# Fused attention and Fourier-mixing kernel: V's two signs in one tile, heads in natural order, stores as steps of their own, and a new order of work

## The chip, the cores and the metric

The kernel runs on one core of a Trainium2 chip, in one launch. A core has five engines with queues of their own: TensorE (PE, with its weight loads shown as PEld), VectorE (DVE), ScalarE (ACT), GpSimd (POOL) and SyncE (SP). SP, ACT and POOL also issue DMAs. Each engine works through its own queue in the order in which the program was written, and waits for others by semaphores. The metric is the device time of one execution, in microseconds (us), lower is better; what is compared is the median of several runs.

## What is computed

Inputs are q, k and v, each 8 batches x 8 heads x 576 rows x 64, a projection `w_phi` (64 x 128), and two feed-forward weights (512 x 2048 and 2048 x 512), all fp32.

```python
def phi(x):
    proj = np.einsum('bhsd,df->bhsf', x, w_phi)
    proj = proj - np.max(np.abs(proj), axis=-1, keepdims=True)
    return np.concatenate([np.exp(proj), np.exp(-proj)], axis=-1)
q_p, k_p = phi(q), phi(k)
kv = np.einsum('bhsf,bhsd->bhfd', k_p, v);  z = np.sum(k_p, axis=2)
num = np.einsum('bhsf,bhfd->bhsd', q_p, kv)
den = np.einsum('bhsf,bhf->bhs', q_p, z)[..., None] + 1e-06
x = num / den, heads side by side: (8, 576, 512)

mixed = np.real(np.fft.fft(np.fft.fft(x, axis=1), axis=2))
u = x + mixed
un = (u - mean(u)) / sqrt(var(u) + 1e-06)          # over the last axis
out = u + np.maximum(un @ w_ch1, 0.0) @ w_ch2
```

So each batch goes through four parts: feature maps of k and q, linear attention, the real part of a two-dimensional Fourier transform, and a normalised feed-forward network.

## The kernel before

Every batch is a set of small generators ("streams"), each of which issues a few instructions per step. `STREAMS` gives each a letter and a number of steps; the string `PLAN` is the order written out by hand or by a planner: each letter issues the next step of that stream, for its own next batch. So PLAN fixes the order on every engine's queue at once, and steps of neighbouring batches stand interleaved. A step holds instructions of several engines, its DMAs included. Below, `M1.19` means step 19 of stream M for batch 1.

The streams:

- `K`, `V`, `Q` (`fetch_*`, issued on POOL) load a batch of k, v and q, cast to bf16. `B` and `A` (`arrive_k`, `arrive`, on SP) turn k and q by DMA transposes into `KT` and `QT`. Batch 0 instead loads fp32 on SP and turns it on TensorE (`G`, `J`).
- `T` (18 steps; 20 for batch 0) projects k and q (PSUM tiles `psk`, `psh`, `ps`) and exponentiates on ACT into `KPp`, `KPn` (exp(proj), exp(-proj) of k) and `QPHP`, `QPHN`. `R` takes on DVE the maxima of |proj| of k, into `MK` and, for the last 64 rows, `MK4`; `P` those of q into `MQ`.
- `S` puts the factors exp(+max), exp(-max) of k into V: ACT writes the exponential into column 64 of the tile (L438, L424), and POOL multiplies V by it (L443, L428). `VCn`, `VCp` hold the two signs for the first 512 rows, `V4N`, `V4P` for the last 64: one multiply a sign and pair of heads.
- `M` is attention and mixing: `keyvalue` for eight heads (PSUM tile `kv`, ten matmuls a head, then ACT's cast to `kvh`, L861); `combine` for eight heads (TensorE, DVE, and L975 on POOL into `X`); the two Fourier matmul stages (`psD`, then `pu`) with DVE's folded sums into `CEO` between them (L1007, in steps M.17 and M.19); and the sums X + mixed (L1077). `D` folds `X` on DVE before that (L869 to L893).
- `N` normalises: DVE's statistics, ACT's centred bf16 `UN`, then an SP DMA transpose to `UT` (in batch 0 by TensorE). `U` computes 1/sigma (POOL, L1173).
- `F` (68 steps) is the feed-forward network: 128 hidden matmuls (`psf`, L1207) with ACT's Relu eviction into `HT`, then `output` for the five row blocks (`pso`, L1224, L1250), DVE's scaled sum into `X`, and the store.
- `C`, `H` make the Fourier constants, `Z` pads, `W` loads the two weights, `Y` (`stir`) issues filler matmuls in the first part.

The first 512 rows of an X tile lie as four blocks of 128 rows, and c = 4 holds the last 64. The store of a block (`store`, L1180) is called straight after DVE's sum of that block inside `output`:

```python
            nc.vector.scalar_tensor_tensor(
                out=U[:, c, 0:C], in0=po[:], scalar=scale_of[b, c], in1=U[:, c, 0:C], ...
            )
            store(b, U, c)
```

c = 1 stores blocks 0 and 1 by four DMAs on SP's queue, which is also the queue of the transposes of `KT`, `QT` and `UT`.

Heads are taken in pairs, for batch 0 in the order `PAIRS = (0, 3, 2, 1)`, and combined in the order 0, 1, 6, 7, 4, 5, 2, 3. The first two steps of `D` fold `X` by column quarters: first quarters 0 and 3, then 1 and 2.

In batch 0 the q maxima are not applied as a factor afterwards but subtracted inside the projection: `turn_m` (L692) splits 20 maxima a row into three bf16 parts (four small DVE operations), turns them by one matmul, and copies them out of PSUM.

## Time and profile before

| | us |
|---|---|
| median of three runs (lowest, highest) | 416.78 (416.39, 419.95) |
| the profiled execution, its own time | 415.15 |
| its span, first to last instruction | 413.4 |
| TensorE busy in the span | 394.6 (95%) |
| DVE / ACT / POOL busy | 319.4 / 303.8 / 215.1 |
| first hidden-layer matmul of batch 0 | 50.9 |
| last DMA issue (SP) | 408.05 |

The profile is of one execution. "Busy" of TensorE is modelled, as matmuls are pipelined. In a row of groups the columns are: line, engine, operation, output and inputs, shape, count; total busy us and mean ns of one; and idle time ahead of it with what ended it. In a row of waits: engine and line that waited, what ended the wait; total us, times, longest. In a row of the timeline: start, duration, engine, line, operation, and in brackets the idle time before. In a table of stretches, each engine's busy us stands with its instruction count in brackets, and the last columns are granted clock, DMA share and GB/s.

### The profile page before, as it was taken

Reading aid. Unit: us, or ns where it says so; the run is one execution under the profiler, and the core shown is the slowest. Engines: PE = TensorE matmul, PEld = TensorE weight load, DVE = VectorE, ACT = ScalarE, POOL = GpSimd, SP = SyncE. Lnnn points to the kernel's source line nnn. Section 1 sums busy time; section 2 is a strip of 40 time slices with the busy share of each in tenths; the row PEclk is TensorE's granted clock in tenths of the full one; section 3 lists DMA queues with packets and bytes.
Section 4 is the critical chain, followed back from the end, with each engine's and each line's share of the span. In section 5 each row is a group of like instructions: output and inputs, shape, how many; then the busy total and the mean of one; then the engine's idle time right before and its main releaser. Section 6 shows DMA issues by size and latency. Waiting matters only on the chain.

```text
span 413.4 us, 10526 instructions
## 1 busy us (share of the span) xinstructions
PE 394.6 (95%) x4194; PEld 259.5 (63%) x4194; DVE 319.4 (77%) x662; ACT 303.8 (73%) x617; POOL 215.1 (52%) x279
## 2 busy tenths in 40 slices
PE   7898999989999989999899999999999999999994
PEld 3574577535856568566756577566856586658563
DVE  5979887999699867797689878888799768875101
ACT  6988999658958886688868886789758885544350
POOL 8997695774466753707658373649271343201000
PEclk9999899999999999999999999999999999999999
DMA  7999979898674899654965979757952141106103
GB/s 210 221 170 158 181 100 185 87 118 128 102 118 58 67 179 141 63 92 83 129 97 65 156 104 142 80 72 116 117 97 52 46 83 21 27 14 114 24 23 90
DMA packets 108520, 42.71 MB, mean 103 GB/s; under 512 B 82615, under 2 KB 103479, under 8 KB 108471
## 3 DMA queue, kind: packets, MB, share of 16 engines
q0 software_dynamic: 46272, 16.60, 37.1%
q1 hardware_dynamic: 61703, 24.85, 32.9%
q10 hardware_dynamic: 496, 0.59, 0.6%
q8 instruction: 33, 0.54, 0.5%
q14 instruction: 16, 0.13, 0.1%
HBM read 36.77 MB, written 9.44 MB: 112 GB/s over the span
## 4 chain that ended last, share of the span: by engine, by line
PE 69%; DVE 13%; DMA 8%; ACT 4%; POOL 3%; issue 2%; DVEq 0%; POOLq 0%; SPq 0%; ACTq 0%
PE psf L1207 29%; PE pso L1224 19%; DMA UT<-UN 4%; PE kv L853 3%; PE psD L1035 2%; PE psk L468 2%; DMA KT<-KS 2%; PE pu L1087 2%; DMA KS<-in_k_dram 2%; PE psq L522 2%; PE psh L563 1%; DVE MK L488 1%; PE pso L1250 1%; DVE cb L969 1%; DVE X L1077 1%
## 5 line engine op out<-in xcount | busy, mean ns | idle before, releaser
L1207 PE MATMUL psf<-UT,W1b 128*128 128x320 bf16 (+1 forms) x1024 | 141.1, 286 | 2.9 <-DMA UT<-UN 2.8
L1224 PE MATMUL pso<-W2b,HT 128*128 128x512 bf16 x496 | 120.5, 379 | 0.0
L1207 PEld LDWEIGHTS <-W1b 128*128 128x128 bf16 x1024 | 94.6, 98 | 30.9 <-issue 3.8
L1212 ACT ACTIVATE HT<-psf 128x320 bf16<-128x320 f32 x128 | 53.9, 444 | 25.7 <-PE psf L1207 19.5
L1224 PEld LDWEIGHTS <-HT 128*128 128x128 bf16 x496 | 45.2, 98 | 43.2 <-issue 0.4
L975 POOL TENSOR_TENSOR X<-cb,rd 128x640 f32<-128x640 f32 x28 | 35.1, 1254 | 52.9 <-DVE rd L973 29.6
L443 POOL TENSOR_TENSOR VCn<-VS,VCn 128x512 bf16<-128x512 bf16 x28 | 29.9, 1067 | 43.4 <-ACT VCn L438 36.6
L530 DVE TENSOR_REDUCE MQ<-psq 128x8 f32<-128x1024 f32 (+1 forms) x32 | 34.3, 1088 | 17.8 <-PE psq L522 17.4
L1230 DVE SCALAR_TENSOR_TENSOR X<-pso,rs,X 128x512 f32<-128x512 f32 x31 | 23.0, 743 | 28.2 <-PE pso L1224 28.0
L1214 ACT ACTIVATE HT<-psf 128x512 bf16<-128x512 f32 x64 | 37.3, 602 | 6.8 <-PE psf L1207 6.6
L488 DVE TENSOR_REDUCE MK<-psk 128x8 f32<-128x1024 f32 x28 | 33.8, 1210 | 1.4 <-ACT KPn L474 1.4
L474 ACT ACTIVATE KPp<-psk 128x1024 bf16<-128x1024 f32 x28 | 28.8, 1027 | 7.8 <-PE psk L468 7.5
L258 POOL DMA_DIRECT2D QS<-in_q_dram x49 | 33.4, 688 | 1.1 <-issue 1.1
L1133 ACT ACTIVATE UN<-X,MV 128x512 bf16<-128x512 f32 (+1 forms) x35 | 25.2, 726 | 11.5 <-DVE MV L1158 8.0
L572 ACT ACTIVATE QPHP<-psh 128x1024 bf16<-128x1024 f32 x28 | 28.9, 1031 | 4.8 <-PE psh L563 4.5
L474 ACT ACTIVATE KPn<-psk 128x1024 bf16<-128x1024 f32 x28 | 28.7, 1025 | 1.7 <-DVE MK L488 1.6
L443 POOL TENSOR_TENSOR VCp<-VS,VCp 128x512 bf16<-128x512 bf16 x28 | 29.9, 1067 | 0.0
L572 ACT ACTIVATE QPHN<-psh 128x1024 bf16<-128x1024 f32 x28 | 29.0, 1036 | 0.0
L1157 DVE BATCH_NORM_STATS2 st<-X 128x6 f32<-128x512 f32 (+1 forms) x40 | 27.1, 678 | 0.2
L1077 DVE TENSOR_TENSOR X<-pu,X 128x512 f32<-128x512 f32 (+3 forms) x49 | 23.5, 526 | 4.6 <-PE pu L1087 4.5
L955 PEld LDWEIGHTS <-QPHP 128*128 128x128 bf16 x280 | 20.5, 99 | 7.8 <-DVE cb L969 3.8
L1173 POOL TENSOR_TENSOR rs<-VE,mhalf 128x5 f32<-128x5 f32 (+1 forms) x9 | 10.3, 1148 | 24.8 <-DVE VE L1172 24.7
(462 smaller groups left out, 797.2 us busy)
## 6 DMA issues: line engine op xcount, KB each, us to landing
out_dram<-X SPq DMA_DIRECT2D x31, 128.0 KB
out_dram<-X SPq DMA_DIRECT2D x15, 256.0 KB
KS<-in_k_dram POOLq DMA_DIRECT2D x7, 512.0 KB, 8.2
VS<-in_v_dram POOLq DMA_DIRECT2D x14, 256.0 KB, 4.8
...
```

Source lines behind the costliest of these rows:

```text
L258: nc.gpsimd.dma_start(out=pieces[i][0], in_=pieces[i][1])
L443: nc.gpsimd.tensor_tensor(out=VC[:, hs, :, 0:D], in0=values[b][0][:, hs, :].rearrange("p h (j d) -> p h j d", d=D), in1=VC[:, hs, :, D:D + ...
L474: nc.scalar.activation(out=KP[:, hs, :, :].rearrange("p e (jp jj) f -> p jj (e jp) f", jj=2), in_=psk[:], func=AT.Exp, scale=sgn,)
L488: nc.vector.tensor_reduce(out=MK[:, 2 * pr:2 * pr + 2, :].rearrange("p e (jp jj) -> p jj (e jp)", jj=2), in_=tiles[pr][:], axis=AX.X, op=A ...
L530: nc.vector.tensor_reduce(out=o, in_=i[:], axis=AX.X, op=ALU.max, apply_absolute_value=True)
L572: nc.scalar.activation(out=o, in_=psh[:], func=AT.Exp, scale=sgn)
L975: nc.gpsimd.tensor_tensor(out=X[:, :, at:at + 2 * D].rearrange("p c (e d) -> p e c d", e=2), in0=cb[:, :, :, 0:D], in1=rd[:].to_broadcast( ...
L1077: nc.vector.tensor_tensor(out=to, in0=more, in1=to, op=ALU.add)
L1207: nc.tensor.matmul(ps, lhsT=W1b[:, cc, 128 * hh:128 * hh + 128], rhs=UT[:, cc, lo:hi], start=(cc == 0), stop=(cc == NCC - 1),)
L1212: nc.scalar.activation(out=HT[:, hh, lo:hi], in_=ps, func=AT.Relu, scale=-1.0)
L1214: nc.scalar.activation(out=HT[:, hh - 1:hh + 1, lo:hi], in_=psw[:].rearrange("p (a n) -> p a n", a=2), func=AT.Relu, scale=-1.0,)
L1224: nc.tensor.matmul(po[:], lhsT=HT[:, hh, at:at + 128], rhs=W2b[:, hh, :], start=(hh == 0), stop=(hh == NHH - 1),)
```

## The change

1. **V's two signs.** `VCp` and `VCn` become one tile `VC` with a sign axis, `V4P` and `V4N` one tile `V4S`; `MK` and `MK4` get a sign axis too. DVE writes the maxima to sign 1, POOL writes their negatives to sign 0, one ACT exponential covers both signs, and one POOL multiply covers both signs of a pair of heads.
2. **`keyvalue`** uses one PSUM tile for two heads; ACT casts both at once after the second.
3. **Natural head order** in batch 0 and in `combine`; `D`'s first two steps fold column halves. The outer heads' exponentials in batch 0 become one instruction, not two.
4. **q maxima of batch 0** (`turn_m`): ACT copies the fp32 maxima to three places, TensorE transposes them, and DVE splits them into bf16 parts in PSUM.
5. **Rows of X** have 514 elements, not 513.
6. **Stores** become a stream `O` of four steps (five in batch 7), in the order of blocks 2, 1 (with 0), 3, 4.
7. **A new PLAN.** Among other moves: `K1.0` and `K1.1` come ahead of most of S of batch 0; `R1.2` comes before M0.19 instead of after M0.20; `W0.1` comes just before F0.0; S.1 of every later batch comes after M.19; `O` steps lie some steps behind the sums that they store.

The diff, cut:

```diff
-PAIRS = (0, 3, 2, 1)
+PAIRS = (0, 1, 2, 3)
...
-    V4P = const.tile([128, 4, 2, D + 1], BF16, name="V4P")
-    V4N = const.tile([128, 4, 2, D + 1], BF16, name="V4N")
+    V4S = const.tile([128, 2, 4, 2, D + 1], BF16, name="V4S")
...
-        xpool.tile([128, 5, C + 1], F32, tag="X", name=n)[:].rearrange("p a b -> p (a b)")
+        xpool.tile([128, 5, C + 2], F32, tag="X", name=n)[:].rearrange("p a b -> p (a b)")
...
+    def scaling(b, MK, MK4, VC):
+        V, V4_ = values[b]
+
+        def scale_v4():
+            nc.gpsimd.tensor_single_scalar(
+                out=MK4[:, 0], in_=MK4[:, 1], scalar=-1.0, op=ALU.mult
+            )
+            for e in range(2):
+                rr = slice(64 * e, 64 * e + 64)
+                nc.scalar.activation(
+                    out=V4S[rr, :, :, e, D], in_=MK4[rr], func=AT.Exp, scale=1.0
+                )
+                nc.gpsimd.tensor_tensor(
+                    out=V4S[rr, :, :, e, 0:D],
+                    in0=V4_[rr].unsqueeze(1).to_broadcast([64, 2, 4, D]),
+                    in1=V4S[rr, :, :, e, D:D + 1].to_broadcast([64, 2, 4, D]), op=ALU.mult,
+                )
+
+        def scale_v(pr):
+            if pr % 2 == 0:
+                h4 = slice(2 * pr, 2 * pr + 4)
+                nc.gpsimd.tensor_single_scalar(
+                    out=MK[:, 0, h4], in_=MK[:, 1, h4], scalar=-1.0, op=ALU.mult
+                )
+                nc.scalar.activation(
+                    out=VC[:, :, h4, :, D].rearrange("p s h j -> p s (h j)"),
+                    in_=MK[:, :, h4].rearrange("p s h j -> p s (h j)"), func=AT.Exp, scale=1.0,
+                )
+            hs = slice(2 * pr, 2 * pr + 2)
+            to = VC[:, :, hs].rearrange("p s h j d -> p s (h j) d")
+            nc.gpsimd.tensor_tensor(
+                out=to[:, :, :, 0:D],
+                in0=V[:, hs, :].rearrange("p h (j d) -> p (h j) d", d=D).unsqueeze(1)
+                    .to_broadcast([128, 2, 8, D]),
+                in1=to[:, :, :, D:D + 1].to_broadcast([128, 2, 8, D]), op=ALU.mult,
+            )
...
         def turn_m(outer):
...
+            pt = pk.tile([96, 2, 128], F32, tag="pk", name="pt")
+            m = M0w[:, 1 - outer]
+            nc.scalar.copy(out=m[:, 1:3], in_=m[:, 0:1].to_broadcast([128, 2, 32]))
+            nc.tensor.transpose(pt[:, 0], m.rearrange("p i n -> p (i n)"), ident[:])
             mt_ = small.tile([96, 128], BF16, tag="mt", name="mt")
-            nc.vector.tensor_copy(out=mt_[:], in_=pt[:])
+            nc.vector.tensor_copy(out=mt_[:], in_=pt[:, 0])
+            nc.vector.tensor_tensor(
+                out=pt[0:64, 1], in0=pt[0:64, 0], in1=mt_[0:64], op=ALU.subtract
+            )
+            nc.vector.tensor_copy(out=mt_[0:64], in_=pt[0:64, 1])
+            nc.vector.tensor_tensor(
+                out=mt_[0:32], in0=pt[0:32, 1], in1=mt_[0:32], op=ALU.subtract
+            )
...
     def keyvalue(b, h):
...
+        if e == 0:
+            pool, tag = (pb, "pb") if b == 0 else (pk, "pk")
+            two_heads[b] = pool.tile([128, 2, 2, D + 1], F32, tag=tag, name="kv")
+        kv = two_heads[b][:, e]
...
+        if e:
+            kvh = work.tile([128, 2, 2, D + 1], BF16, tag="kvh", name="kvh", bufs=4)
+            nc.scalar.copy(out=kvh[:], in_=two_heads[b][:])
+            return kvh[:, 0], kvh[:, 1]
+        return ()
...
-        for cs in (slice(0, 4, 3), slice(1, 3)):
+        for cs in (slice(0, 2), slice(2, 4)):
...
-        for h in (0, 1, 6, 7, 4, 5, 2, 3):
+        for h in range(H):
             combine(h, kvh[h])
...
-            store(b, U, c)
             yield
...
+    def store_all(b):
+        U = turned_u[b][0]
+        for c in (2, 1, 3, 4) if b < B - 1 else (2, 1, 4):
+            store(b, U, c)
+            yield
+        if b < B - 1:
+            return
+        rows_ = out[b, 320:576, :].rearrange("(a r j) n -> a r j n", r=32, j=2)
+        for queue, at in ((nc.scalar, 0), (nc.sync, 256)):
             queue.dma_start(out=rows_[:, ::-1, 0, at:at + 256], in_=U[:, 3, at:at + 256])
             yield
```

More of the change, by code (lines that the diff above doesn't have):

```diff
@@ L243, in pads @@
             yield
-        for X_ in (V4P, V4N):
-            nc.gpsimd.memset(X_[:], 0.0)
+        for sgn in range(2):
+            nc.gpsimd.memset(V4S[:, sgn], 0.0)
             yield
@@ L339, in load_first, with half @@
         parts[0] = first_features()
+    def half(x, outer):
+        return x[:, 0:2] if outer else x[:, 2:4]
     def turn_part(dst, blocks, by_act):
@@ L679, in last_rows @@
             if sgn < 0:
-                for x, pr in enumerate((0, 3) if outer else (1, 2)):
+                for x, pr in enumerate((0, 1) if outer else (2, 3)):
                     for e in range(2):
@@ L721, in widest @@
                 nc.vector.tensor_reduce(
-                    out=half(by_pair(mq[:])[:, :, :, c], outer),
+                    out=M0[:, 1 - outer, :, :, c],
                     in_=ps[jj][:].rearrange("p (x e) f -> p x e f", e=2), axis=AX.X, op=ALU.max,
@@ L842, in first_features @@
+            for pr in range(4):
+                yield scale_v(pr)
         return maxima(), steps(), kmax(), scaled()
     def keyvalue(b, h):
-        KPp, KPn, K4p, K4n, VCp, VCn, _ = made[b]
+        KPp, KPn, K4p, K4n, VC, _ = made[b]
         pr, e = h // 2, h % 2
-        if b == 0:
-            kv = pb.tile([128, 2, D + 1], F32, tag="pb", name="kv")
-        else:
-            kv = pk.tile([128, 2, D + 1], F32, tag="pk", name="kv")
-        for i, (KP, K4, VC, V4) in enumerate(((KPp, K4p, VCp, V4P), (KPn, K4n, VCn, V4N))):
+        if e == 0:
+            pool, tag = (pb, "pb") if b == 0 else (pk, "pk")
+            two_heads[b] = pool.tile([128, 2, 2, D + 1], F32, tag=tag, name="kv")
@@ L857, in keyvalue @@
             nc.tensor.matmul(
-                kv[:, i, :], lhsT=K4[:, pr, :], rhs=V4[:, pr, e, :], start=False, stop=True
+                kv[:, i, :], lhsT=K4[:, pr, :], rhs=V4S[:, i, pr, e, :], start=False, stop=True
             )
-        kvh = work.tile([128, 2, D + 1], BF16, tag="kvh", name="kvh", bufs=8)
-        nc.scalar.copy(out=kvh[:], in_=kv[:])
-        return kvh
+        if e:
[3 more added lines that the diff above has]
+        return ()
     def folded(X, R, HI):
@@ L926, in first_heads @@
             for e in range(2):
-                kvh[2 * pr + e] = keyvalue(0, 2 * pr + e)
+                for x, made_ in enumerate(keyvalue(0, 2 * pr + e)):
+                    kvh[2 * pr + x] = made_
                 yield
-        for h in (0, 1, 6, 7):
+        for h in range(4):
             ps = pb.tile([128, 1, 512], F32, tag="pb", name="pn_")
@@ L941, in heads @@
             return (yield from first_heads())
-        KPp, KPn, K4p, K4n, VCp, VCn, E2 = made[b]
-        X = xpool.tile([128, 5, C + 1], F32, tag="X", name="X")
+        E2 = made[b][5]
+        X = xpool.tile([128, 5, C + 2], F32, tag="X", name="X")
         R = fpool.tile([128, 3, 2, 512], F32, tag="R", name="R")
@@ L1261, in forward @@
             )
-        store(b, U, 4)
         yield
@@ L1265, in forward @@
             return
-        rows_ = out[b, 320:576, :].rearrange("(a r j) n -> a r j n", r=32, j=2)
-        for queue, at in ((nc.scalar, 0), (nc.sync, 256)):
+        for at in (0, 256):
             po = pb.tile([128, 256], F32, tag="pb", name="pso")
```

178 lines of the change are left out of this document (50 added, 128 removed).

## The prediction

> **What bounds the kernel now.** I read the page's totals first, then busy time by stage. The stage bounds are the starts, in the chain of waits, of the first hidden-layer matmul of batch 0 (50.9), batch 1 (104.6) and batch 7 (375.8).
>
> ```profile
> PE 394.6 (95%) x4194; PEld 259.5 (63%) x4194; DVE 319.4 (77%) x662; ACT 303.8 (73%) x617; POOL 215.1 (52%) x279
> ```
> ```profile
> core 0: us, PE busy (x) PEld busy (x) DVE busy (x) ACT busy (x) POOL busy (x), PEclk, DMA share, GB/s
> 0.00:50.90 50.90, 44.07 (x493) 25.75 (x493) 42.27 (x103) 44.36 (x84) 43.01 (x75) 0.97 1.15 188
> 50.90:104.60 53.70, 51.53 (x582) 32.77 (x582) 48.70 (x101) 43.57 (x90) 37.16 (x44) 1.00 0.95 122
> 104.60:375.80 271.20, 267.28 (x2885) 179.31 (x2883) 221.22 (x448) 202.52 (x419) 133.76 (x160) 1.00 0.64 90
> 375.80:413.40 37.60, 31.70 (x240) 21.64 (x238) 7.25 (x15) 13.36 (x27) 1.17 (x1) 0.99 0.29 58
> ```
>
> From 104.6 to 375.8, six batches at 45.2 us, TensorE idles 271.20 - 267.28 = 3.92 us in all. The last stage is bare feed-forward matmuls. Their count is the same after the change, so what can move is the idle: 3.92 us here, 2.17 us from 50.9 to 104.6, and the start, where TensorE's busy time is partly the filler matmuls of `stir`. There ACT is busy 44.36 of 50.9 us, DVE 42.27 and POOL 43.01: three nearly full engines bound it. Matmul ends are modelled, so some waits may hide inside "busy"; that goes into the range.
>
> Then the waits, to see what the idle is (us in total, times, longest):
>
> ```profile
> PE psf L1207 <- DMA UT<-UN: 2.8, 4, 1.3
> PE psk L468 <- DMA KT<-KS: 1.8, 1, 1.8
> PE psD L1035 <- DVE CEO L1007: 1.2, 1, 1.2
> ...
> PE psD L1035 <- DVE CEO L1053: 0.4, 1, 0.4
> ...
> POOL VCn L443 <- ACT VCn L438: 36.6, 8, 12.5
> ...
> SPq L1184 <- DVE X L1230: 60.9, 6, 15.0
> ...
> SPq L1150 <- ACT UN L1133: 36.1, 7, 14.0
> ```
>
> TensorE waits for the transposed activations `UT` at four batch starts, for K once, and for DVE's `CEO` once. POOL, 52% busy, stands waiting for ACT's exponentials.
>
> **V's two signs in one tile.** Rows by form:
>
> ```profile
> L443 POOL TENSOR_TENSOR VCn<-VS,VCn 128x512 bf16<-128x512 bf16 x28 | 29.9, 1067 | 43.4 <-ACT VCn L438 36.6 <-issue 2.8 <-ACT VCp L438 2.7
> ...
> L428 POOL TENSOR_TENSOR V4N<-VS,V4N 64x256 bf16<-64x256 bf16 x14 | 8.7, 618 | 22.4 <-ACT V4N L424 18.5 <-PE psf L1207 3.4
> ...
> L438 ACT ACTIVATE VCn<-MK 128x16 bf16<-128x16 f32 x14 | 4.0, 287 | 0.4 <-DVE MK L488 0.3
> ...
> L424 ACT ACTIVATE V4N<-MK 64x4 bf16<-64x4 f32 x14 | 3.0, 216 | 0.4 <-DVE MK L483 0.2
> ...
> L861 ACT CAST kvh<-kv 128x130 bf16<-128x130 f32 x64 | 17.4, 276 | 2.7 <-PE kv L857 2.6
> ...
> L1024 ACT CAST ET<-psD 128x289 bf16<-128x289 f32 x2 | 0.8, 426 | 0.0
> ...
> L509 POOL COPY MQ<-MQ 64x4 f32<-64x4 f32 x7 | 1.6, 230 | 5.4 <-DVE MQ L506 5.1
> ```
>
> Per batch, ACT issues two exponentials fewer for V (2 x 287) and two fewer for its last rows (2 x 216): -1.0 us. Four `kvh` casts of 260 elements replace eight of 130. Between 276 ns (130) and 426 ns (289) a cast of 260 takes 0.40, so 4 x 0.40 - 8 x 0.276 = -0.6. ACT: -1.6 us a batch.
> POOL: 618 ns (256 elements) and 1067 (512) extend to an estimated 1.97 us for 1024. Four of those replace eight of 1.067 (-0.66), two of 1.067 replace four of 0.618 (-0.34), and three sign flips are new, nearest the 230 ns copy (+0.7; at the 618 ns of the small multiply +1.9): POOL -0.3, off the path. The one-buffer PSUM tile `kv` is handed over four times a batch, not eight; no wait above names it: 0.
> The new wait is ACT's exponential on POOL's flip. Behind it on ACT stand the PSUM evictions, and TensorE waits for those. In 8 of the V steps POOL had already been standing for ACT, up to 12.5 us, so a flip would be long done. I take 0; the dearer end is the rival "hop".
> What 1.6 us less of ACT is worth in the middle: ACT is busy 202.5 of 271.2 us and TensorE idles 3.92. I take -2.5 us over batches 1 to 6 (between 0 and -3.9).
>
> **Order and heads, batch 0.** The chain before 50.9:
>
> ```profile
> 26.34 6.46 DMA KS<-in_k_dram
> 32.94 7.08 DMA KT<-KS
> ...
> 48.12 1.14 DVE MK L488
> ...
> 50.90 2.34 PE psf L1207 x20
> ```
> ```profile
> 37.92 0.39 PE L994 MATMUL pm<-HI,ones_b 128*128 128x512 bf16 x1
> 40.07 0.40 PE L468 MATMUL psk<-wphi,KT 64*128 64x128 bf16 x8 [1.76 <-DMA KT<-KS]
> ...
> 39.56 1.03 DVE L1007 TENSOR_TENSOR CEO<-R 128x384 bf16<-128x384 f32 x2
> ...
> 46.55 0.69 DVE L1072 SCALAR_TENSOR_TENSOR X<-pu,X 128x512 f32<-128x512 f32 x1 [0.98 <-PE pu L1087]
> ```
>
> In the new order K's load (`K`) stands ahead of the V multiplies (`S`) on POOL, so the 1.76 us wait for `KT` goes. But the next matmul needs `CEO`, and DVE ends that at 39.56 + 1.03 = 40.6: DVE is late next, worth 0 (at best -1.8). The third K-maximum (`R`) moves ahead of the first spectrum add, where DVE idles 0.98 us, instead of standing in the chain at 48.12: 1.14 - (1.14 - 0.98) = -0.98, less a later start of that add by 0.1: -0.9. ACT also loses work here:
>
> ```profile
> L639 ACT ACTIVATE QPHP<-psh 128x512 bf16<-128x512 f32 x4 | 2.3, 662 | 0.0
> ...
> L648 ACT ACTIVATE QPHP<-psh 128x1024 bf16<-128x1024 f32 x2 | 2.1, 1070 | 0.0
> ```
>
> Four outer exponentials become one instruction each: up to 2 x 0.662 - 1.070 = 0.25 a time, some 0.8; with the V part that is -2.4, plus two new copies for the q maxima, about 0.23 each (as the 230 ns copy): -2.0. The engine being 87% full, I count half: -1.0. W1's load moves ahead of three column-constant steps on POOL and meets the v loads still running on SP's queue; V's rows are first needed by POOL, nearly full here: 0, at worst +2. Start: -1.9 (from -5 to +2).
>
> **q maxima split in PSUM.**
>
> ```profile
> 20.69 0.34 DVE L696 CAST m<-MQ 128x20 bf16<-128x20 f32 x1
> ...
> 21.28 0.38 DVE L698 CAST m<-ml 128x20 bf16<-128x20 f32 x1
> ...
> 22.69 0.29 DVE L706 CAST mt<-pt 96x128 bf16<-96x128 f32 x1 [0.82 <-PE pt L701]
> ```
>
> The old way takes 22.69 + 0.29 - 20.69 = 2.3 us end to end, twice, in batch 0. The new one is a copy, a transpose and four DVE passes of 128 columns at about 0.29: 1.9 us with the hand-overs. -0.4 each at most and beside ACT's exponentials: 0.
>
> **V multiplies moved past the folds.** Batch 1 has the largest idle of TensorE after 50.9:
>
> ```profile
> 91.19 1.88 DVE L1007 TENSOR_TENSOR CEO<-R 128x381 bf16<-128x381 f32 x2
> ...
> 91.41 1.25 POOL L443 TENSOR_TENSOR VCn<-VS,VCn 128x512 bf16<-128x512 bf16 x1
> 92.63 1.36 POOL L443 TENSOR_TENSOR VCp<-VS,VCp 128x512 bf16<-128x512 bf16 x1
> ...
> 93.00 1.03 DVE L1053 CAST CEO<-R 128x6 bf16<-128x6 f32 x1
> ...
> L1007 DVE TENSOR_TENSOR CEO<-R 128x381 bf16<-128x381 f32 x8 | 4.4, 556 | 0.3
> ```
>
> DVE's pair took 1.88 us where two mean ones take 1.11, POOL's multiplies 1.25 and 1.36 where the mean is 1.067, all overlapping: they slow each other. In the old order `S2.1` stands before DVE's step `M1.19`; in the new one every batch's first V multiply (`S.1`) stands after `M.19`. That removes the two `psD` waits, 1.2 + 0.4: -1.6 us (between 0 and -1.9).
> The Trainium skill, "SBUF — State Buffer", section "SBUF: two separate sides", says a GpSimd operation and a VectorE operation with two SBUF inputs take a shared port for the whole instruction, and the loser blocks; here the trace agrees (1.88 against 1.11 us), and by that rule the doubled multiply is a longer block, the rival "port".
>
> **Stores.** On SP's queue at a batch start:
>
> ```profile
> 143.45 1.58 SPq L1184 DMA_DIRECT2D out_dram<-X  x2
> 145.40 2.81 SPq L1150 DMA_TRANSPOSE UT<-UN  x2
> ```
>
> The four-DMA store of two row blocks ends just before the transposes start, and those wait for ACT's `UN` (36.1 us), not for the store. In the new order the same store (`O.1`) still mostly precedes `N.0`. I take 0; if a late store now stands in front of a ready `UN`, it costs up to four issues, 4 x 0.79 = 3.2 us a batch. In the last batch the two final stores go out on two queues when their data is ready, as now: 0. X rows of 514 and the column halves change no element count: 0 (±0.5).
>
> **Sum.** The profiled execution took 415.15 us (span 413.4 and 1.75 around it). -1.9 - 1.6 - 2.5 = -6.0 gives 409.15. The median of the three runs, 416.78, lies 1.63 above the profiled one, so I forecast 410.8.
>
> **Rivals.**
> *Relief off the path* (0.26): 95% TensorE says ACT's saving ends as ACT idle. Then about a third of the sum stays: -2, so 414.8.
> *All visible waits go* (0.12): 2.17 + 3.92 and the start's -5 make -11: 405.7. For it speaks that each wait is a different small one; against, that the new order can make others.
> *Port* (0.08), slower: multiplies of 1.97 us meet a DVE fold once a batch and hold it that long, and `psD` waits as at 91 us, 1.5 us each: 7 x 1.5 = 10.5, less the -1.9 of the start, +8.6: 425.4. It decides from about 0.9 us a batch (6.0 / 7). Against: `S.1` stands behind `M.19`.
> *Hop* (0.08), slower: the flip for heads 4 to 7 queues behind two multiplies (3.9 us) and ACT stands for it. One multiply's worth a batch, 7 x 1.97 = 13.8, three quarters of it felt (ACT is 75% busy): +10.3 - 3.5 = +6.8: 423.6. Against: POOL's idle before these steps.
> *It does not do what it says* (0.04): the stores leave in the same order and nothing moves: 416.8.
> My forecast holds 0.42.
>
> **How the numbers follow.** About 1% (4.2 us) is what a measurement of this kernel tells from no change. Faster than 412.6: most of the forecast (0.37), all of the second rival (0.12) and a little of the first (0.03): 0.52. Slower: the two slower rivals, less what falls inside 1%, 0.15. Within: 0.33. The forecast's own range, from its bounds, is 406 to 414; for 8 in 10 it reaches down past the second rival to 404 and up through the first to 418.5.
>
> **What would show it.** Right: first hidden matmul near 49; no `psD` wait on `CEO` in batch 1; ACT some 11 to 13 us less busy; `UT` waits no longer than now. Wrong: ACT's V exponentials waiting on a POOL flip, L1007's successor with a mean well above 0.57 us, SP's transposes behind a store, or a start no earlier than 50.9.

## The result: slower by 1.6%

| | before | after |
|---|---|---|
| median, us (13 runs each) | 416.53 | 421.61 |
| ratio, with its 95% interval | | 1.0158 [1.0133, 1.0183] |
| profiled execution, us | 415.15 | 420.94 |
| span, us | 413.4 | 419.2 |
| first hidden-layer matmul of batch 0 | 50.9 | 61.25 |
| of batch 0 to batch 1 | 53.7 | 52.0 |
| of batch 1 to batch 7 | 271.2 | 268.85 |
| from there to the end | 37.6 | 37.1 |

The ratio is taken from the fast executions alone and is not the quotient of the two medians, which is 1.012. The forecast was 410.8. The rest of the kernel gained about as much as was forecast for it, and the start lost 10.35 us.

### The profile after

The page's totals of the kernel after, and its busy time by the same four stages as in the prediction:

```profile
PE 394.8 (94%) x4166; PEld 260.8 (62%) x4194; DVE 318.0 (76%) x660; ACT 298.3 (71%) x551; POOL 213.2 (51%) x255
```
```profile
core 0: us, PE busy (x) PEld busy (x) DVE busy (x) ACT busy (x) POOL busy (x), PEclk, DMA share, GB/s
0.00:61.25 61.25, 47.83 (x493) 27.63 (x493) 43.14 (x102) 43.92 (x72) 42.79 (x72) 0.89 0.94 154
61.25:113.25 52.00, 51.73 (x608) 33.81 (x610) 47.18 (x101) 42.95 (x80) 38.81 (x44) 1.00 0.97 128
113.25:382.10 268.85, 263.76 (x2836) 177.56 (x2856) 221.57 (x450) 199.21 (x376) 130.45 (x140) 1.00 0.72 88
382.10:419.20 37.10, 31.52 (x240) 21.76 (x240) 6.09 (x12) 12.26 (x25) 1.17 (x1) 0.95 0.30 76
```

The first row is the whole loss. ACT, DVE and POOL did the same work there as before (43.92 against 44.36 us, 43.14 against 42.27, 42.79 against 43.01), but in 61.25 us instead of 50.9: all three stood still for about ten microseconds more. TensorE was granted a clock of 0.89 there, where it had 0.97 (1.00 is full speed). The other rows are shorter than before.

What they stood for is seen in the chain of waits of the kernel after (start, duration, what), the part before its first hidden-layer matmul:

```profile
10.27 13.07 DMA HT<-in_v_dram
23.50 0.44 POOL V4S L421
...
25.80 0.34 ACT VC L433
```

and in POOL's timeline of the kernel after:

```profile
7.70 0.99 POOL L91 DMA_DIRECT2D W1b<-in_moe_w_ch_dram  x1
...
14.09 0.24 POOL L413 TENSOR_SCALAR MK<-MK 128x4 f32<-128x4 f32 x1
22.27 1.05 POOL L421 TENSOR_TENSOR V4S<-HT,V4S 64x512 bf16<-64x512 f32 x1 [7.94 <-DMA HT<-in_v_dram]
```

v of batch 0 takes 13 us from its issue at 10.27 to its landing. POOL stands idle for 7.94 us waiting for it, and ACT behind POOL. In the kernel before, POOL started that multiply at 14.13. W1's load is issued at 7.70, while it was issued at 12.93 before. The DMA queues between 10 and 20 us, before (packets, MB, share of the 16 engines' time; q1 is the queue of SP's loads, q0 that of POOL's):

```profile
q1 hardware_dynamic: 2551, 1.53, 55.1%
q0 software_dynamic: 168, 0.69, 40.0%
```

and in the same ten microseconds after:

```profile
q0 software_dynamic: 459, 1.88, 93.4%
q1 hardware_dynamic: 944, 0.27, 15.6%
```

SP's loads (the last of q, and v) moved 0.27 MB where they had moved 1.53. W1 had the engines. Nothing needs W1 before the first hidden-layer matmul; the next multiply on POOL needs v.

The waits of TensorE in the kernel after (total us, times, longest), the rows that answer to those quoted of before:

```profile
PE kv L821 <- POOL VC L439: 2.9, 1, 2.9
...
PE pn__4741 L926 <- DVE MK L502: 2.0, 1, 2.0
PE psD L990 <- DVE CEO L978: 1.9, 2, 1.2
...
PE ps L468 <- ACT HT L1185: 0.9, 1, 0.9
```

The 2.8 us of waits for `UT` are gone, and so is K's 1.8. Both `psD` waits that are left stand in batch 0. New in the batches is the 2.0 us before a combining matmul of batch 5 (`pn__4741`).

### The profile page after: what moved, and what is told of

Its sections match the earlier page's. It is cut to its first block, busy times and chain, and to the rows that moved or that the text cites. A ratio compares the mean times of both kernels' runs of the same rounds, so it can differ in the third digit from the quotient of the medians.

```text
span 419.2 us, 10386 instructions
## 1 busy us (share of the span) xinstructions
PE 394.8 (94%) x4166; PEld 260.8 (62%) x4194; DVE 318.0 (76%) x660; ACT 298.3 (71%) x551; POOL 213.2 (51%) x255
## 4 chain that ended last, share of the span: by engine, by line
PE 80%; ACT 5%; DVE 5%; DMA 4%; issue 2%; POOL 1%; SPq 1%; DVEq 0%; POOLq 0%; ACTq 0%
PE psf L1178 29%; PE pso L1195 22%; PE kv L821 4%; PE pso L1220 4%; DMA HT<-in_v_dram 3%; PE psD L1006 3%; PE pu L1058 2%; PE psq L536 2%; PE idle L1300 2%; PE psh L577 2%; PE psk L482 2%; DMA wphi_f<-in_w_phi_dram 1%; SPq L312 1%; DVE cb L940 1%; DVE tg L933 1%
## 5 line engine op out<-in xcount | busy, mean ns | idle before, releaser
L1195 PE MATMUL pso<-W2b,HT 128*128 128x512 bf16 x468 | 117.4, 380 | 1.6 <-issue 0.5
L1183 ACT ACTIVATE HT<-psf 128x320 bf16<-128x320 f32 x128 | 53.5, 439 | 30.3 <-PE psf L1178 24.6
L439 POOL TENSOR_TENSOR VC<-VS,VC 128x1024 bf16<-128x1024 bf16 x28 | 53.6, 1932 | 28.4 <-ACT VC L433 23.4
L544 DVE TENSOR_REDUCE MQ<-psq 128x8 f32<-128x1024 f32 (+1 forms) x32 | 34.3, 1085 | 12.4 <-PE psq L536 12.3
L421 POOL TENSOR_TENSOR V4S<-VS,V4S 64x512 bf16<-64x512 bf16 x14 | 14.7, 1052 | 33.4 <-ACT V4S L418 32.9
```

What stands on the lines that cost most here:

```text
L439: nc.gpsimd.tensor_tensor(out=to[:, :, :, 0:D], in0=V[:, hs, :].rearrange("p h (j d) -> p (h j) d", d=D).unsqueeze(1) .to_broadcast([128, ...
L544: nc.vector.tensor_reduce(out=o, in_=i[:], axis=AX.X, op=ALU.max, apply_absolute_value=True)
L1183: nc.scalar.activation(out=HT[:, hh, lo:hi], in_=ps, func=AT.Relu, scale=-1.0)
L1195: nc.tensor.matmul(po[:], lhsT=HT[:, hh, at:at + 128], rhs=W2b[:, hh, :], start=(hh == 0), stop=(hh == NHH - 1),)
```

## The experiments

Times below are medians, with the ratio to the kernel before on the same chip. The kernels ran on several chips, on which the kernel before took 415.3 to 416.5 us, so small differences are judged by the ratios and their intervals. "F0" is the start of the first hidden-layer matmul of batch 0, from TensorE's timeline; F1 to F7 are those of the later batches. Each F comes from one profiled execution. Where two kernels have the same start, F0 differed by up to 0.7 us: 53.81 and 54.54 (`e1_w_behind`, `e7_stores_straight`), 53.44 and 52.88 (`e4_old_start`, `e8_v6_behind`). `PLAN` is shown only where it differs. The theory after seeing the result: one letter of the order, W's first, costs the start its ten microseconds. The rivals: V's sign flips and longer multiplies cost it, or the other moves do.

### W's first load put back, later, early in the old kernel, and halved

`e1_w_behind`, the changed kernel with one letter moved:

```diff
-    "YYCCZZYGGGTCTZGGTRZWRJKCTTTSPRTYJJRKJSPTYPTSTRYMPJMSTPMTSMTQTQQPTMMMPMTTVMMZMCTTMTHHDMVBMDHDYYYYHDYA"
+    "YYCCZZYGGGTCTZGGTRZRJKCWTTTSPRTYJJRKJSPTYPTSTRYMPJMSTPMTSMTQTQQPTMMMPMTTVMMZMCTTMTHHDMVBMDHDYYYYHDYA"
```

> The changed kernel with one letter of the order moved: the first load of W (W1, 4 MB, on POOL's software queue) goes behind the step C0.3 with its three column-constant instructions, as it stands in the kernel before, so that it is issued at about 12.5 us instead of 7.70. Theory (W1's load takes the DMA engines while v and the last q still run on SP's queue, and holds them back until 22 us): v lands by about 16 us, POOL's V4S multiply no longer waits 7.9 us, the first hidden-layer matmul starts at 49 to 52 us instead of 61.3, and the time is about 421.6 - 10.4 = 411 us, under both kernels. Rival (the start is late because ACT's V exponentials wait for POOL's sign flips and for the longer two-sign multiplies): the first hidden-layer matmul stays beyond 57 us and the time above 417.

Measured: F0 53.81, 414.6 us, ratio 0.9971 [0.9936, 1.0006]. Moving this letter back takes 7.4 us off the start and 7 to 8 off the time (7.0 by the medians, 7.8 by the ratios). The expected 411 was too good: F0 is still 2.9 us later than in the kernel before.

`e1b_w_late`, the same letter further back:

```diff
-    "YYCCZZYGGGTCTZGGTRZWRJKCTTTSPRTYJJRKJSPTYPTSTRYMPJMSTPMTSMTQTQQPTMMMPMTTVMMZMCTTMTHHDMVBMDHDYYYYHDYA"
+    "YYCCZZYGGGTCTZGGTRZRJKCTTTSPRTYJJRKJSPTYPTSWTRYMPJMSTPMTSMTQTQQPTMMMPMTTVMMZMCTTMTHHDMVBMDHDYYYYHDYA"
```

> The changed kernel with the first load of W moved further back, behind the step S0.2, that is behind both loads of k of batch 1 on POOL's queue and behind the first V multiplies. Theory: as with W behind C0.3, v is not held back, so the first hidden-layer matmul starts at 49 to 52 us and the time is about 411; W1 takes about 17 us and is there before 50 if it is issued before 30. If W1's own arrival or the loads queued behind it (q and v of batch 1) set something, this kernel differs from the one with W behind C0.3 by over 2 us. Rival (sign flips and two-sign multiplies delay the start): first hidden-layer matmul beyond 57, time above 417.

Measured: F0 54.7, 417.42, ratio 1.0045 [1.0018, 1.0071]. The start is within 0.9 us of the other, and the trace shows 1.6 us of loss between F4 and F5. TensorE does not wait longer there: its busy time is 46.37 us against 44.77, at a granted clock of 0.97 against 1.00. Over ten runs each, the median of the granted clock is 0.984 against 0.991. Why the clock is lower with a later W1 is not shown.

`e2_before_w_early`, the kernel before with W1's load early and nothing else of the change:

```diff
-    "CYCCZYCYGGTRTTGZZGTYZWRTJTSRJGRJYSTPTSPKTTPJMJRTSSKMYMBMPTQPTPQVTMZTMQTMMTPCMMMTTMTHDYAMMYHHDHHKYYVD"
+    "CYCCZYWCYGGTRTTGZZGTYZRTJTSRJGRJYSTPTSPKTTPJMJRTSSKMYMBMPTQPTPQVTMZTMQTMMTPCMMMTTMTHDYAMMYHHDHHKYYVD"
```

> The kernel before with one letter of its order moved: the first load of W goes ahead of the step C0.3, so that it is issued at about 6.5 us instead of 12.93; nothing else of the change. Theory: the loads on SP's queue that are still running (the last q, v) fall to about a tenth of their rate until W1 is through, v lands beyond 20 us instead of by 16, the first hidden-layer matmul starts 6 to 12 us later than its 50.9, and the time is 422 to 428. Rival (it is the changed kernel's sign flips, two-sign multiplies, heads in natural order or its other early steps that delay its start): no change, 416.5 within 2.

Measured: F0 62.14 (+11.2), 425.79 (four runs), ratio 1.0231 [1.015, 1.0311]. The profiled execution was the longest of the four, 431.73 us, so the 11.2 is an upper value. Its waits between 8 and 40 us:

```profile
POOL V4N L818 <- DMA HT<-in_v_dram: 9.3, 1, 9.3
...
PE pst L345 <- DMA HT<-in_q_dram: 9.2, 1, 9.2
```

The old code, with none of the new flips, tiles or heads, loses at least as much by this one letter as the whole change costs (1.0231 against 1.0158; the intervals overlap). W1 was issued at 6.29 us there, 1.4 earlier than in the changed kernel.

`e10_half_w`, half of the suspected cause: the changed kernel with W1 in two loads, the first where the change has it, the second behind S0.2.

```diff
-        nc.gpsimd.dma_start(out=W1b[:], in_=moe_w_ch1.rearrange("(j p) h -> p j h", p=128))
-        yield
+        W1_ = moe_w_ch1.rearrange("(j p) h -> p j h", p=128)
+        for js in (slice(0, 2), slice(2, 4)):
+            nc.gpsimd.dma_start(out=W1b[:, js], in_=W1_[:, js])
+            yield
```

> The changed kernel with its first load of W cut in two halves of W1's rows: one half stays where the change put it (issued at 7.7 us), the other is issued behind the step S0.2. Half the suspected cause, all else equal. Theory (the bytes of W1 in front of v hold v back): the load holds the DMA engines for some 5 us instead of 10, v lands about 5 us earlier, the first hidden-layer matmul starts about half way between the 53.8 with W behind and the 61.2 of the changed kernel, at 56 to 59, and the time is 416.5 to 419.5. Rival (not the bytes but the issue on POOL, or the changed steps beside it): first hidden-layer matmul beyond 60, time above 420.

Measured: F0 57.17, 418.48, ratio 1.0056 [1.0026, 1.0086]. POOL's wait in it:

```profile
POOL V4S L423 <- DMA HT<-in_v_dram: 4.6, 1, 4.6
```

No byte, half and all of W1 ahead of v give F0 at 53.81, 57.17 and 61.25, and POOL waits for v of 0, 4.6 and 7.9 us. The loss goes with the bytes. That settles the cause of 7.4 of the 10.35 us.

### Code and order apart

`e3_old_order` is the changed code under the old PLAN, with O steps put in behind the sums. In batch 0 the store of block 2 came to stand ahead of its sums, so that block is stored unfinished. The first lines of its PLAN:

```diff
-    "YYCCZZYGGGTCTZGGTRZWRJKCTTTSPRTYJJRKJSPTYPTSTRYMPJMSTPMTSMTQTQQPTMMMPMTTVMMZMCTTMTHHDMVBMDHDYYYYHDYA"
+    "CYCCZYCYGGTRTTGZZGTYZWRTJTSRJGRJYSTPTSPKTTPJMJRTSSKMYMBMPTQPTPQVTMZTMQTMMTPCMMMTTMTHDYAMMYHHDHHKYYVD"
...
```

> The code of the changed kernel under the order of the kernel before, with each store step right behind the sums that it stores, as before. Theory (the loss lies in the order, in one letter of it): W1 is issued at about 13 us, the first hidden-layer matmul starts at 50 to 52, and the rest of the code gives ACT's relief, estimated at up to 2.5 us: 413 to 417. Rival (the code itself, V's flips and two-sign multiplies, delays the start): first hidden-layer matmul at 55 or later and a time above 420.

Measured: F0 55.8, 427.07, ratio 1.0276 [1.0198, 1.0355]. By both its marks the rival was right: even with W behind, the new code under the old order starts late and is slower than either kernel. What makes its start late was not taken apart. But its trace shows what the prediction's rival "port" described. The old order has V's first multiplies of batch 2 (S2.1) in front of DVE's step M1.19, and now they are two-sign. DVE's timeline and POOL's:

```profile
97.62 2.75 DVE L978 TENSOR_TENSOR CEO<-R 128x381 bf16<-128x381 f32 x2
100.29 1.90 DVE L1024 CAST CEO<-R 128x6 bf16<-128x6 f32 x1
```
```profile
97.65 4.51 POOL L439 TENSOR_TENSOR VC<-VS,VC 128x1024 bf16<-128x1024 bf16 x2 [0.46 <-ACT VC L433]
```

Beside the doubled multiplies DVE's pair takes 2.75 us, where it took 1.88 beside the single ones of the kernel before, and a cast of six elements a row takes 1.90, where the mean of the kernel after is 0.17. TensorE waits 2.0 and 0.9 us for `CEO` here, and 1.2 and 0.4 in the kernel before.

`e5_before_code` is the old code under the new PLAN (W behind C0.3, no O). Batch 1's head 6 is combined one step before its last query features are written (T1.17 stands behind M1.10, which is head 2 in the new code), so it takes rows of the batch before.

```diff
-    "CYCCZYCYGGTRTTGZZGTYZWRTJTSRJGRJYSTPTSPKTTPJMJRTSSKMYMBMPTQPTPQVTMZTMQTMMTPCMMMTTMTHDYAMMYHHDHHKYYVD"
+    "YYCCZZYGGGTCTZGGTRZRJKCWTTTSPRTYJJRKJSPTYPTSTRYMPJMSTPMTSMTQTQQPTMMMPMTTVMMZMCTTMTHHDMVBMDHDYYYYHDYA"
...
```

> The code of the kernel before (V's signs in tiles of their own, heads 0 1 6 7, kvh casts one by one, stores inside the sums' steps, rows of 513) under the changed order, with W's first load behind C0.3 and without the store steps. Theory (what the changed kernel gains behind the start, some 4 us between the first hidden-layer matmuls of batches 0 and 7, is ACT's relief and so the code's): 2.5 to 4 us slower than the changed code under this order, 417 to 418.6. Rival (that gain is the order's): 414.6 within 1, or less if the code's flips cost at the start.

Measured: F0 59.7, 448.48, ratio 1.0789 [1.0732, 1.0846]. Its waits of TensorE begin with

```profile
PE kv L853 <- ACT kvh L861: 23.8, 25, 2.4
```

The single PSUM tile `kv` is handed over eight times a batch in the old code, and the new order puts these eight steps close together: 25 of them wait for ACT's cast of the head before. So the new order seems to need the new code's pairs of heads; this is read from the waits and was not tried by itself. Neither half can be priced alone by leaving the other out, and "the gain lies in the code" and "in the order" are both wrong as put.

`e4_old_start`: the changed code; its first 43 steps in the old order, then the new order for all the others. Against `e1_w_behind`:

```diff
-    "YYCCZZYGGGTCTZGGTRZRJKCWTTTSPRTYJJRKJSPTYPTSTRYMPJMSTPMTSMTQTQQPTMMMPMTTVMMZMCTTMTHHDMVBMDHDYYYYHDYA"
+    "CYCCZYCYGGTRTTGZZGTYZWRTJTSRJGRJYSTPTSPKTTPKJRYMPJMSTPMTSMTQTQQPTMMMPMTTVMMZMCTTMTHHDMVBMDHDYYYYHDYA"
```

> The changed code whose order begins as that of the kernel before (its first 43 steps, up to P0.2, with W's first load at about 13 us, the memsets of V's and Q's pads on POOL behind C0.2 and C0.3, and each K maximum next to its matmuls), and goes on as that of the changed kernel for all other steps. With W behind C0.3 alone, the first hidden-layer matmul stood at 53.8, 2.9 us later than the 50.9 of the kernel before, with DVE's L186 at 2.35 us instead of 0.94 and the first K maximum of DVE at 12.10 instead of 9.33. Theory (that rest is the new order's: pads in front of DVE's constants, casts of K in front of the K maxima): first hidden-layer matmul at 50 to 52, time about 412. Rival (the rest is the code's: V's sign flips, the two-sign multiplies, the split of the maxima): it stays at 53 to 54.5 and the time at 414.6 within 1.

Measured: F0 53.4, 412.5, ratio 0.9937 [0.9912, 0.9963]. The first K maximum came back to 9.59 us from 12.10, but F0 moved by only 0.4, no more than it differs between executions of one start: most of what this removed had slack. By F0 the rival was right. By the time the theory was, but the intervals of the two kernels overlap.

### Two parts undone

On `e1_w_behind`. `e6_signs_apart` undoes V's common exponentials and multiplies:

```diff
-            nc.gpsimd.tensor_single_scalar(
-                out=MK4[:, 0], in_=MK4[:, 1], scalar=-1.0, op=ALU.mult
-            )
-            for e in range(2):
...
+            for sgn, i in ((1.0, 1), (-1.0, 0)):
+                for e in range(2):
...
```

> The changed kernel with W's first load behind C0.3, and V's two signs apart again: no sign flip on POOL, two exponentials with scale 1 and -1 on ACT, two multiplies of half the size on POOL; all else (pairs of kvh casts, natural heads, order, stores) as changed. Theory (ACT's relief is what pays in the batches): ACT is busy about 1 us a batch more and the time goes to 415.5 to 417. If the relief is off the path: 414.6 within 0.8. Rival (the flip's hop from ACT to POOL and back costs at the start): first hidden-layer matmul earlier than 53 and the time below 413.8.

Measured: F0 55.7, 416.63, ratio 1.0001 [0.9958, 1.0043]; ACT busy 302.0 instead of 298.3. Undone, the kernel is 2.0 us slower by the medians, but the intervals overlap, and the traces do not put the loss down to ACT alone. Stage by stage, from one F to the next, the two profiles agree within 0.3 us up to F7, but for F0, 1.9 later, and F4 to F5, 2.6 longer. That stage with the signs together and apart, in the columns of the table of stages above:

```profile
241.89:289.09 47.20, 44.77 (x483) 29.70 (x483) 37.02 (x75) 37.66 (x70) 24.32 (x26) 1.00 0.75 96
```
```profile
243.46:293.26 49.80, 46.50 (x482) 30.28 (x482) 38.00 (x77) 38.89 (x75) 25.32 (x30) 0.97 0.68 91
```

TensorE is busy 1.7 us longer there, at a granted clock of 0.97 instead of 1.00, and waits 0.9 us for `UT`. At the start it reaches the first K matmul of batch 1 at 41.26 us against 41.11, so taking the flip away gains nothing under this order. Of the later F0, 0.6 us lie in front of a `pu` matmul that stands behind POOL's multiply of V's last rows, and most of the rest in a stretch from 50 to 54 us with a granted clock of 0.50 to 0.76. In the other batches undoing the relief changed nothing, so that ACT's relief pays there is not shown.

`e7_stores_straight` puts each O step right behind the sums that it stores. Batch 0's, as an example of all:

```diff
-    "FUMFFVTMBTFFMFMFMFMVFMATFRFPDTFDFTKKFFDQFFDRTFFFFFSMFTQFFFFVFRTMFFTFRFQFOFFMMTFSFFMRFTFOSTTMNMFFSFNM"
+    "FUMFFVTMBTFFMFMFMFMVFMATFRFPDTFDFTKKFFDQFFDRTFFFFFSMFTQFFFFVFRTMFFOTFRFQFFFMMTFSFFOMRFTFSTTMNMFFSFNM"
```

> The changed kernel with W's first load behind C0.3, and each store step right behind the step that makes its sums, as in the kernel before; all else as changed. Theory (stores 0, off the path): 414.6 within 1. Rival (a store that waits for its sums on SP holds the transposes of the next batch behind it, up to 3.2 us a batch): 417 or more.

Measured: 417.9, ratio 1.0051 [1.0005, 1.0098], against 414.6 and 0.9971 with the stores late: 3.3 us by the medians, with intervals that just touch. SP's timeline of this kernel at the start of a batch:

```profile
172.63 0.61 SPq L1161 DMA_DIRECT2D out_dram<-X  x1
188.21 2.59 SPq L1155 DMA_DIRECT2D out_dram<-X  x4
190.90 1.23 SPq L388 DMA_TRANSPOSE KT<-KS  x1
192.24 3.28 SPq L390 DMA_TRANSPOSE KT<-KS  x2
195.61 2.56 SPq L1121 DMA_TRANSPOSE UT<-UN  x2
```

and of the one with late stores:

```profile
172.95 1.78 SPq L388 DMA_TRANSPOSE KT<-KS  x1
182.13 2.63 SPq L390 DMA_TRANSPOSE KT<-KS  x2
187.80 2.59 SPq L1155 DMA_DIRECT2D out_dram<-X  x4
191.23 2.85 SPq L1121 DMA_TRANSPOSE UT<-UN  x2
```

With the store straight behind the step of its sums, SP stands from 173.2 to 188.2 for it, and the transposes of the next batch's K, which the other kernel does between 173 and 185, queue behind. They then run when `UT`'s turn would be, and `UT` is issued 4.4 us later, though ACT's `UN` is only 0.4 later. TensorE's wait in this kernel:

```profile
PE psf L1178 <- DMA UT<-UN: 2.0, 1, 2.0
```

F2 to F3, the stage that ends with this wait, takes 47.3 us against 45.2. F3 to F4 takes 49.8 against 44.9: a second wait of 3.3 us before a hidden matmul, at 210 us, has no releaser in the profile and stays unexplained, and TensorE is busy 1.6 us longer at a granted clock of 0.97 instead of 1.00. The profiled execution, 420.96 us, is the longest of its ten. So the mechanism is shown, for one batch and 2 us; its share of the 3.3 us is not.

### DMA issues on POOL ahead of its arithmetic

The 2.0 us wait of a combining matmul in batch 5 (`pn__4741` in most) stands in every kernel so far that has the new order there. Around it in `e4_old_start`, POOL's timeline and DVE's:

```profile
254.68 1.26 POOL L946 TENSOR_TENSOR X<-cb,rd 128x640 f32<-128x640 f32 x1 [0.82 <-DVE rd L944]
255.88 2.13 POOL L258 DMA_DIRECT2D VS<-in_v_dram  x3
258.03 1.27 POOL L946 TENSOR_TENSOR X<-cb,rd 128x640 f32<-128x640 f32 x1
```
```profile
259.33 1.29 DVE L839 TENSOR_TENSOR R<-X 128x512 f32<-128x512 f32 x2 [2.58 <-POOL X L946]
...
261.80 1.22 DVE L502 TENSOR_REDUCE MK<-psk 128x8 f32<-128x1024 f32 x1
```

`e8_v6_behind` is this kernel with the steps that issue these loads moved behind the multiply:

```diff
-    "FPTNUMFFMFFMFMFFMVFMVFAMFFFTTTDRTFFTFFFSFFFFRMFFOFFKMFFFFFRDTFFQFFDKFFFFDRTMTMFFTFFMMFFSFRMFTTSTFMFV"
+    "FPTNUMFFMFFMFMFFMFMFMVVAFFFTTTDRTFFTFFFSFFFFRMFFOFFKMFFFFFRDTFFQFFDKFFFFDRTMTMFFTFFMMFFSFRMFTTSTFMFV"
```

> The kernel with the old start (412.5), and in batch 5 the two steps that load v of batch 6 (V6.0, V6.1, three DMA issues on POOL, 2.13 us) moved from in front of the step M5.13 to behind it; A6.0, which needs them, follows. Theory (the issues stand in front of X's multiply L946, so DVE's fold L839 idles 2.58 us with the K maximum queued behind it, and a combining matmul waits 2.16 us for the PSUM tile that this maximum frees): that wait at 260.7 us goes and the time is 410.0 to 411.5. Rival (the wait is set by DVE's work or ACT's, and the time comes back as another wait in the batch): 412.5 within 0.7.

Measured: 411.72, ratio 0.9896 [0.9865, 0.9926]; DVE's idle 2.58 became

```profile
256.49 1.29 DVE L839 TENSOR_TENSOR R<-X 128x512 f32<-128x512 f32 x2 [1.37 <-POOL X L946]
```

and TensorE's wait 0.8 instead of 2.0. But the stage ends with a wait that was not there:

```profile
PE psf L1178 <- DMA UT<-UN: 1.2, 1, 1.2
```

F4 to F5 takes 47.2 us, against 47.4 in `e4_old_start`: in this execution the time came back as another wait, as the rival said. Three of the later kernels with this move do not have the new wait, and there the stage takes 45.9 (`e9_p5_ahead`, `e12_k1_behind`, `e13_first_apart`); `e11_copy_dve` has it, and takes 47.1. So the move does take its wait away, and is worth from 0.2 to 1.4 us by execution. The median, 411.72 against 412.5, lies just above the expected 410.0 to 411.5, and the intervals overlap.

`e9_p5_ahead` adds a move at the start:

```diff
-    "CYCCZYCYGGTRTTGZZGTYZWRTJTSRJGRJYSTPTSPKTTPKJRYMPJMSTPMTSMTQTQQPTMMMPMTTVMMZMCTTMTHHDMVBMDHDYYYYHDYA"
+    "CYCCZYCYGGTRTTGZZGTYZWRTJTSRJGRJYSTPTSPKTTPKJRYMPJMSTPMTSMPTQTQQTMMMPMTTVMMZMCTTMTHHDMVBMDHDYYYYHDYA"
```

> As the kernel with V6 behind M5.13, and at the start the step P0.5 (a q maximum) ahead of T0.12 instead of behind T0.13. In the kernel with the old start DVE idles some 1.9 us before that maximum, whose matmuls stand behind T0.12 and T0.13 on PE. Theory (that maximum sets the second transposed row of maxima, whose matmul stood at 28.96 against 27.59 in the kernel before): the first hidden-layer matmul moves from 53.4 to 52 to 52.8 and the time falls by 0.5 to 1.3 against the kernel with V6 behind. Rival (something else sets the first combining at 30.6, ACT's exponentials for one): no difference within 0.4.

Measured: F0 53.38, against 52.88 in `e8_v6_behind` and 53.44 in `e4_old_start`; 411.55, ratio 0.9900 [0.9876, 0.9925]. No difference: the rival. DVE's idle ahead of that maximum was slack.

### What still makes the start late

`e11_copy_dve` is `e9_p5_ahead` with

```diff
-            nc.scalar.copy(out=m[:, 1:3], in_=m[:, 0:1].to_broadcast([128, 2, 32]))
+            nc.vector.tensor_copy(out=m[:, 1:3], in_=m[:, 0:1].to_broadcast([128, 2, 32]))
```

> The kernel with V6 behind and P0.5 ahead (411.55), and the copy of the q maxima in turn_m on DVE instead of ACT. In that kernel the second such copy starts on ACT at 28.59, behind two QPHN exponentials and a cast, though its maxima are there at 26.55; the matmul that transposes them starts at 28.89, against 27.59 in the kernel before, where the split ran on DVE alone. Theory (this queue behind ACT's exponentials is a part of the 2.5 us by which the first hidden-layer matmul is still later than before): the second transposing matmul comes at 27 to 27.5, the first hidden-layer matmul at 51.8 to 52.6 instead of 53.4, and the time falls by 0.7 to 1.4, to about 410.5. Rival (V's multiplies on POOL, which end at 27.6, hold the same place): no difference within 0.4.

Measured: F0 53.5, 411.82, ratio 0.9897 [0.985, 0.9944]; the second transposing matmul did not move (29.0). The copy was not what it waited for: TensorE reaches it in its own order, straight behind the `kv` matmuls and with no idle time in front.

`e12_k1_behind` is that kernel with K1.0 and K1.1 behind S0.4:

```diff
-    "CYCCZYCYGGTRTTGZZGTYZWRTJTSRJGRJYSTPTSPKTTPKJRYMPJMSTPMTSMPTQTQQTMMMPMTTVMMZMCTTMTHHDMVBMDHDYYYYHDYA"
+    "CYCCZYCYGGTRTTGZZGTYZWRTJTSRJGRJYSTPTSPTTPJRYMPJMSTPMTSKKMPTQTQQTMMMPMTTVMMZMCTTMTHHDMVBMDHDYYYYHDYA"
```

> As the kernel with that copy on DVE, and the two loads of k of batch 1 (K1.0, K1.1, 1.67 us of DMA issues on POOL at 21.3, between V's multiplies) behind the last of V's multiplies of batch 0. Theory (DMA issues in front of POOL's arithmetic delay what waits for it): V's last multiply ends at about 25.9 instead of 27.6, the first hidden-layer matmul starts 0.8 to 1.6 earlier than with the copy alone, the time falls by as much. Rival (V's multiplies aren't on the path of the start): no difference within 0.4, or a loss where k of batch 1 comes later.

Measured: F0 53.5, 412.04, ratio 0.9908 [0.9875, 0.994]. V's last multiply ended at 28.1, no earlier than the 27.6 of `e9_p5_ahead`: POOL, with the loads out of its way, stood 2.07 us for ACT's second V exponential. Two causes fell. What the trace of `e9_p5_ahead` shows of ACT's waits between 8 and 40 us, the longest:

```profile
ACT VC L433 <- POOL MK L430: 1.5, 1, 1.5
```

`e13_first_apart` takes that flip away, in batch 0 alone (`scaling_apart` holds the exponentials and multiplies of `e6_signs_apart`):

```diff
-        scale_v4, scale_v = scaling(0, MK, MK4, VC)
+        scale_v4, scale_v = scaling_apart(0, MK, MK4, VC)
```

> The kernel with V6 behind and P0.5 ahead (411.55), with V's two signs apart again in batch 0 alone (no sign flip on POOL; exponentials with scale 1 and -1, as in the kernel before), two-sign tiles and flips in batches 1 to 7. In that kernel ACT stands for 1.50 us ahead of V's first exponential at 17.13, waiting for the flip MK L430, which is queued on POOL behind the 2.18 us of V4S; the fourth KPn exponential ends at 20.14 instead of 18.94. Theory (the rest of the start's delay is this hop from ACT to POOL and back): that wait goes, the fourth KPn ends at about 19, the first hidden-layer matmul starts at 51.8 to 52.6 instead of 53.4, and the time falls by 0.8 to 1.6, to about 410.3. Rival (ACT makes it up, or PSUM tiles hold PE at the same place): first hidden-layer matmul within 0.4 of 53.4 and no difference in the time.

Measured: F0 52.17, 410.62, ratio 0.9845 [0.9789, 0.9900]. The wait is gone, the fourth KPn exponential ends at 18.94 as before, and F0 comes 1.2 us earlier than in `e9_p5_ahead`, as the theory said (0.7 to 1.3 earlier than in the five kernels that begin much like it and have the flip). So ACT's hop to POOL costs about 1 us under the old start, while under the changed order `e6_signs_apart` gained nothing at the start without it. The intervals of the times overlap (0.9845 against 0.9900), so the time alone would not show it.

The last 1.3 us against 50.9 are open. One candidate was not tried: the filler matmuls of `stir`. Between the last combining matmuls of batch 0 and the first K matmul of batch 1 stand, before and in this kernel:

```profile
33.25 4.26 PE L1322 MATMUL idle<-ones_b 128*128 128x512 bf16 x16
```
```profile
34.07 5.34 PE L1334 MATMUL idle<-ones_b 128*128 128x512 bf16 x20
```

The new order has one group of four more there, 1.1 us, which the kernel before has in front of those combining matmuls. The chain of waits of this kernel runs through all five groups.

This kernel beats both: 1.5% under the kernel before, and 2.6% under the changed one by the medians.

## Why the prediction was wrong

**The step that failed** is a single term: "W1's load moves ahead of three column-constant steps on POOL and meets the v loads still running on SP's queue; V's rows are first needed by POOL, nearly full here: 0, at worst +2". The collision was seen and priced at the wrong size. With W1 behind, POOL waits 0 us for v; with it in front, it waits 7.9, and F0 is 7.4 us later, up to 11.2 in the old code. Two things were wrong in the reasoning. No number was given for how two queues share the engines: they went 1.88 MB to 0.27, so v all but stopped. And it took "POOL is nearly full" as cover, though a nearly full engine has no slack to hide a wait in: POOL stood 7.9 us, and F0 came 7.4 later.

**The rest of the start** was also forecast too well, and without W it is still 53.8, not 49. K's wait for `KT` went, as said, and DVE's `CEO` was late next, as said (1.9 us). ACT's relief there, counted at half of 2.0 us, was smaller: it is busy 43.7 us up to F0 in `e1_w_behind`, where it was 44.4. The hoisted K maximum, counted at -0.9, has no run of its own, so what it gained is open; but it did not fall into an idle gap. DVE's timeline of the kernel after has it straight in front of the first spectrum add:

```profile
56.36 1.23 DVE L502 TENSOR_REDUCE MK<-psk 128x8 f32<-128x1024 f32 x1 [0.42 <-ACT KPn L488]
57.50 0.68 DVE L1043 SCALAR_TENSOR_TENSOR X<-pu,X 128x512 f32<-128x512 f32 x1
```

It waits there for ACT's exponential and holds the add behind it. Of the rival "hop", put at 0.08 and priced through all batches, there is a piece at the start: about 1 us (`e13_first_apart`). In the batches ACT's V exponentials hardly wait for flips. Their row in the kernel after, and ACT's one long wait, at 25.8 us, which v caused:

```profile
L433 ACT ACTIVATE VC<-MK 128x32 bf16<-128x32 f32 x16 | 5.6, 351 | 4.8 <-POOL MK L430 4.8
```
```profile
ACT VC L433 <- POOL MK L430: 3.9, 1, 3.9
```

That leaves 0.9 us for the others of this row; the exponentials of V's last rows wait 1.2 us for their flips, in two places.

**V multiplies past the folds**, -1.6: batch 0 to batch 1 went from 53.7 to 52.0, and no `psD` wait is left in batch 1. Every kernel with the new code and the new order has these 52.0. Right, and `e3_old_order`, with the multiplies in front of the folds, shows the wait that this move avoids.

**ACT's relief**, -2.5 over batches 1 to 6: 271.2 became 268.85, -2.35. The size is right by luck. From F1 on, the six stages changed by -1.6, -1.4, -1.6, +1.4, +1.8 and -1.0 us: a sum of gains and losses, where the forecast had one steady gain. And with V's half of the relief undone (`e6_signs_apart`), the four stages that gained are as short as with it. So that half did not bring these gains; whether the casts in pairs or the order did is open. ACT's busy time fell by 5.5 us, not 11 to 13. The row sums did fall by that: V's exponentials from 16.1 to 9.3 and the casts from 17.4 to 12.4, 11.8 in all. The casts after:

```profile
L830 ACT CAST kvh<-kv 128x260 bf16<-128x260 f32 x32 | 12.4, 386 | 2.6 <-PE kv L825 2.2
```
But small instructions overlap on ACT, as the kernel before shows:

```profile
51.57 0.28 ACT L438 ACTIVATE VCn<-MK 128x16 bf16<-128x16 f32 x1
51.68 0.27 ACT L438 ACTIVATE VCp<-MK 128x16 bf16<-128x16 f32 x1
51.78 0.72 ACT L1127 ACTIVATE UN<-X,nm 128x512 bf16<-128x512 f32 x1
```

Each lasts 0.28 us, but the next starts after 0.11. The sum used durations where the distance of starts was wanted. Two things in these stages the forecast did not have: the late stores, worth 2 us in one batch of the trace and 3.3 by the medians (`e7_stores_straight`), and the loads issued in front of `X`'s multiply, which took 0.2 to 1.4 us back (`e8_v6_behind`).

**Stores**, 0: probably wrong, and the trace of before did show where to look. The forecast asked whether a late store can stand in front of `UT`, and found that `UT` waits for `UN`. It did not ask what an early store, standing on SP for its sums, holds behind it: the transposes of K.

**q maxima**, 0 and 1.9 us end to end: from the copy at 28.70 to the last DVE pass it took 1.9, and `e11_copy_dve` moved nothing. **The two-sign multiply**, estimated at 1.97 us, took 1.93:

```profile
L439 POOL TENSOR_TENSOR VC<-VS,VC 128x1024 bf16<-128x1024 bf16 x28 | 53.6, 1932 | 28.4 <-ACT VC L433 23.4
```

**The rival "port"** did not come, because the first V multiplies stand behind M.19, the reason that the prediction gave against it: the `CEO` rows' mean is 0.555 us after and 0.556 before. Under the old order it does come (`e3_old_order`).

"Wrong" was to show by a start no earlier than 50.9, and it did.
